# SyncE's issue order in two stretches of a one-core training step: stores between the late transposes of x, and transposes of phi(k) and dq around those of dk

## The chip, the core and the metric

The kernel runs on one NeuronCore of a Trainium2 chip. A core has five engines with a queue of instructions each: TensorE (PE, matrix multiplies, with its weight loads shown apart as PEld), VectorE (DVE), ScalarE (ACT), GpSimd (POOL) and SyncE (SP). SyncE computes nothing: it issues DMAs. An engine works through its queue in order, and an instruction whose semaphores are not there yet holds up all that stands behind it. The metric is the device time of one execution in microseconds (us); less is better.

## The reference

The step is the forward and backward pass of one pre-norm block with S = 2048 tokens, width D = 640, 32 heads of 20, and a feed-forward width F = 1728. Cut to what matters:

```python
phi = lambda t: jnp.where(t > 0, t + 1, jnp.exp(t)) + 1e-6
def A(x):                                   # linear attention
    q, k, v = heads(x @ wqkv)
    kv, z = sum_s(phi(k) v^T), sum_s(phi(k))
    return merge((phi(q) @ kv) / (phi(q) @ z + 1e-6)) @ wo
def B(x):                                   # gated feed-forward
    return (silu(x @ w_gate) * (x @ w_up)) @ w_down
h  = x + A(layernorm(x))
h2 = h + B(layernorm(h))
# returned: h2 and the gradients of x, wqkv, wo, w_gate, w_up, w_down for a given grad_out
```

Two products matter here. In the forward pass k and q come from `xn @ wqk`, where xn is the normalised x. In the backward pass the gradient of xn is a sum of three products, `dxn = dq @ Wq^T + phi(k) @ WV2 + dk @ Wk^T`. TensorE contracts over the partitions, so the left factor of each product is needed transposed (features on the partitions, tokens along the row): xnT for the first, dqT, pkT and dkT for the second.

## The kernel before, in words

The tokens are cut into 16 tiles of 128 (ST = 16), the width into 5 blocks of 128 (DT = 5). A result of one tile is 128x640, made in two halves of 320 columns (`NCH`). A manual schedule fixes the order of the code for all five engines in the first stretch below, and for SyncE and VectorE in the second; a scheduler orders the other engines there.

**The first stretch (lines 268 to 401).** For each tile t the kernel normalises x (`ln1_stats`, `ln1_xn` on VectorE and GpSimd), transposes it, and multiplies it by the k and q weights (`kq_mm`, line 299, with 20 matmuls a tile on line 305). Tiles 0 to 7 are transposed on TensorE (`ln1_tr`, `ln1_tr1`) and copied out. Tiles 8 to 15 are transposed by a DMA that SyncE issues: in the loop over t (line 369) the step t normalises tile t + 3 and issues its transpose (line 378). Between these transposes SyncE issues what the table `queue` (line 328) lists for step t, after that step's work: `load_dh2T` transposes rows of grad_out (lines 227 and 228), `store_q`, `store_k` and `store_x` write four tiles each of phi(q), phi(k) and xnT to DRAM for later stages (lines 319 to 326), and `load_wv`, `load_wo` and `load_wdT` fetch weights. One store moves 640 KB.

**The second stretch (lines 825 to 972).** Before its loop SyncE transposes weights (`wqkvT`, lines 840 and 745), and TensorE makes the rest of a sum for the attention output (`ps_gt`), the weight gradients `dwqk(0, i)` (line 883) and, in `wk2` (line 877), the five blocks of the matrix WK2, which SyncE transposes into WV2 (line 881). A buffer `ring` holds ten transposed tiles: four slots for dkT, three for pkT, three for dqT. `load_pqT(v)` (line 873) issues two DMA transposes, phi(k) of tile v from DRAM into slot 4 + v % 3 and dq of tile v from SBUF into slot 7 + v % 3:

```python
def load_pqT(v):
    nc.sync.dma_start_transpose(out=ring[:, 4 + v % 3], in_=scr_pk[v * P:(v + 1) * P, :])
    nc.sync.dma_start_transpose(out=ring[:, 7 + v % 3], in_=dq[v // 8][:, v % 8, :])
```

Lines 896 and 897 call it for tiles 0, 1 and 2 before any of that. The loop of line 927 then runs t from 0 to 18. At t < 16 it makes dk of tile t (`ps_dk`, ten matmuls through `mm_row` on line 109, finished on VectorE in lines 938 and 940) and issues its transpose on SyncE (line 941). Three steps later (LAG = 3, u = t - 3) it makes dxn of tile u (line 964): for each half five matmuls with dqT, five with pkT against WV2, and five with dkT, 30 in all. After them `load_pqT(u + 3)` reuses the slots just read (line 967). In the steps t = 2 and t = 3 stand also `dwqk(0, 3)` and `dwqk(0, 4)`. The layer norm's backward (`ln_bwd`) and the store of dx follow each dxn.

Everything else (the feed-forward's forward and backward pass, its weight gradients, the attention's backward pass, and the last products that make h2) is not touched.

Of the kernel before, what the change touches and what calls it, by code (L numbers as in the profile page):

```python
# [20 lines left out]
def kernel(  # L21
# [41 lines left out]
    def mm(name):  # L63

        return psum.tile([P, 2, 512], FP32, name=name, tag="mm")

    def row(ps):
        return ps[:, :, :320]

    def half(ap):  # L70
        return ap.rearrange("p (c n) -> p c n", c=2)
# [3 lines left out]
    def wk(name, w=D, pool=0):  # L75
        return wpools[pool].tile([P, w], BF16, name=name, tag="w", padded_shape=[P, D])
# [28 lines left out]
    def mm_row(ps, lhs, rhs, n, start=True, stop=True):  # L105

        for ci in range(2):
            for k in range(n):
                nc.tensor.matmul(ps[:, ci, :320], lhsT=lhs(k), rhs=rhs(k, *NCH[ci]),  # L109
                                 start=(start and k == 0), stop=(stop and k == n - 1))  # L110
# [31 lines left out]
    def ln_bwd(ps, xhat, rstd_col, resid, dst, pool):  # L142
        sums = small.tile([P, 2], FP32, name="lb_s", tag="lb_s")
        dy = wk("lb_dy", pool=pool)
        nc.scalar.activation(out=half(dy[:]), in_=row(ps), func=ACT.Copy, scale=rstd_col, accum_out=sums[:, 0:1])  # L145
        a = wk("lb_a", pool=pool)
        nc.vector.tensor_tensor_reduce(out=a[:], in0=dy[:], in1=xhat, scale=1.0, scalar=0.0,  # L147
                                       op0=ALU.mult, op1=ALU.add, accum_out=sums[:, 1:2])
        k = small.tile([P, 2], FP32, name="lb_k", tag="lb_k")
        nc.vector.tensor_scalar(out=k[:], in0=sums[:], scalar1=-1.0 / D, scalar2=None, op0=ALU.mult)  # L150
        nc.scalar.activation(out=a[:], in_=xhat, func=ACT.Identity, scale=k[:, 1:2], bias=k[:, 0:1])
        nc.vector.tensor_tensor(out=a[:], in0=a[:], in1=dy[:], op=ALU.add)
        nc.vector.tensor_tensor(out=dst, in0=a[:], in1=resid, op=ALU.add)
# [16 lines left out]
    def stage():  # L170
        return small.tile([P, 7, P], BF16, name="stg", tag="stg", bufs=3)
# [153 lines left out]
    def store_x(c):  # L325
        nc.sync.dma_start(out=scr_xnT[4 * c:4 * c + 4].rearrange("t p k c -> p t k c"), in_=xnT[:, 4 * c:4 * c + 4])

    queue = {4: [(load_dh2T, 0)], 5: [(store_q, 0)], 6: [(store_x, 0)], 7: [(load_dh2T, 512, 256)], 9: [(store_q, 1), (load_dh2T, 768, 256)],
             10: [(store_x, 1)], 11: [(store_k, 0)], 12: [(load_dh2T, 1024), (store_k, 1)], 13: [(store_x, 2), (load_wv,)],
             14: [(store_q, 2), (load_wo, 0, HG), (store_x, 3), (load_dh2T, 1536)],  # L330
             15: [(store_k, 2), (load_wdT, wdT, 1), (store_k, 3), (load_wdT, wdT3, 3)]}

# [139 lines left out]
    with tc.manual_schedule(engines={EngineType.PE, EngineType.DVE, EngineType.SP, EngineType.Pool}):  # L472
# [86 lines left out]
        for t in range(ST + 2):  # L559
# [19 lines left out]
            while h1_todo and h1_todo[0][0] < t:  # L579
                v, h1 = h1_todo.pop(0)  # L580
# [244 lines left out]
    with tc.manual_schedule(engines={EngineType.SP, EngineType.DVE}):  # L825
# [7 lines left out]
        def load_pk(t):  # L833
            pkrs[t] = small.tile([P, D], BF16, name="pkr", tag="stg", bufs=3, padded_shape=[P, 7 * P])
            nc.gpsimd.dma_start(out=pkrs[t][:], in_=scr_pk_v[:, t, :])
# [3 lines left out]
        def tr_cols(dst, src, c):  # L839
            nc.sync.dma_start_transpose(out=dst.unsqueeze(1), in_=src[:, c:c + P])  # L840
# [32 lines left out]
# [3 lines that stand above are left out]
# [7 lines left out]
        def dwqk(which, i, between=None):  # L883
            ev = wk("dwqk", pool=i % 2)
            ps = mm("ps_dwqk")
            for ci, (n0, n1) in enumerate(NCH):
                for t in range(ST):
                    nc.tensor.matmul(ps[:, ci, :320], lhsT=xn_r[:, t, i * P:(i + 1) * P],  # L888
                                     rhs=dq[t // 8][:, t % 8, n0:n1] if which == 0 else dk[:, t, n0:n1],
                                     start=(t == 0), stop=(t == ST - 1))  # L890
                if between and ci == 0:
                    between()
            nc.scalar.copy(out=half(ev[:]), in_=row(ps))
            nc.gpsimd.dma_start(out=out_2[i * P:(i + 1) * P, which * D:(which + 1) * D], in_=ev[:])

        for v in range(3):
            load_pqT(v)
        for t in range(ST):
            nc.vector.tensor_scalar(out=xn_r[:, t, :], in0=xn_r[:, t, :], scalar1=mv1[:, t, 0:1],
                                    scalar2=rstd1[:, t:t + 1], op0=ALU.subtract, op1=ALU.mult)  # L900
# [21 lines left out]
        def load_mT(t):  # L922
            if t % 4 == 0:
                mTs[t // 4] = strips.tile([P, 4, FT, P], BF16, name="mT", tag="S")
            nc.sync.dma_start_transpose(out=mTs[t // 4][:, t % 4], in_=scr_m[t * P:(t + 1) * P, :])

        for t in range(ST + LAG):
            if t in (2, 3):
                dwqk(0, t + 1)
            if t < ST:  # L930
                if t + 2 < ST:
                    load_pk(t + 2)
                pkr = pkrs.pop(t)
                nc.vector.tensor_scalar(out=pkr[:], in0=pkr[:], scalar1=-1e-6, scalar2=1.0, op0=ALU.add, op1=ALU.min)
                tk = wk("tk", pool=1)
                ps = mm("ps_dk")
                mm_row(ps, lambda i: xnT_r[:, t, i, :], lambda i, n0, n1: WK2[:, i, n0:n1], DT)
                nc.vector.scalar_tensor_tensor(out=half(tk[:]), in0=row(ps), scalar=rstd1[:, t:t + 1] if t < NC else 1.0,
                                               in1=half(dzb[:]), op0=ALU.mult, op1=ALU.add)
                nc.vector.tensor_tensor(out=dk[:, t, :], in0=tk[:], in1=pkr[:], op=ALU.mult)  # L940
                nc.sync.dma_start_transpose(out=ring[:, t % 4], in_=dk[:, t, :])
            if 8 <= t < 8 + HG:
                tr_cols(G[:, t - 8, :], scr_GT, OH[t - 8])
            if t == 14:
                nc.sync.dma_start_transpose(out=KV.rearrange("p j c -> p (j c)").unsqueeze(1), in_=scr_KVT)
            if t == ST:
                dKV = stage()[:, :HG, :]
                nc.sync.dma_start_transpose(out=dKV, in_=dKVT.rearrange("p j c -> p (j c)"))
            if t == ST:
                wd = big.tile([P, FT, D], BF16, name="wd", tag="B")  # L950
                nc.sync.dma_start(out=wd[:, :13, :], in_=B_w_down[0:13 * P, :].rearrange("(j p) d -> p j d", p=P))
                for r in (0, 64):
                    nc.sync.dma_start(out=wd[r:r + 64, 13, :], in_=B_w_down[13 * P:F, :])
            u = t - LAG
            if u < 0:
                continue
            if t >= ST:
                dwqk(1, t - ST)
            pkT, dqT, dkT = ring[:, 4 + u % 3], ring[:, 7 + u % 3], ring[:, u % 4]
            ps = mm("ps_dxn")  # L960
            for ci, (n0, n1) in enumerate(NCH):
                for k, (lhs, rhs) in enumerate(((dqT, wqkvT[:, 0:5]), (pkT, WV2), (dkT, wqkvT[:, 5:10]))):
                    for i in range(DT):
                        nc.tensor.matmul(ps[:, ci, :320], lhsT=lhs[:, i, :], rhs=rhs[:, i, n0:n1],  # L964
                                         start=(k == 0 and i == 0), stop=(k == 2 and i == DT - 1))
            if u + 3 < ST:
                load_pqT(u + 3)
            if ST - MTA <= u:
                load_mT(u - ST + MTA)
            dx = wk("dx")  # L970
            ln_bwd(ps, xn_r[:, u, :], rstd1[:, u:u + 1], dh1[:, u, :], dx[:], 0)
            nc.gpsimd.dma_start(out=o1_v[:, u, :], in_=dx[:])
# [120 lines left out]
```

## Time and profile before

| | |
|---|---|
| time, median of 4 runs | 813.49 us (812.93 to 815.82) |
| the profiled execution (one of the four) | 815.82 us |
| its span, first to last instruction | 814.1 us |
| granted TensorE clock | 1.000 |
| TensorE busy | 806.3 us (99%) |
| VectorE, ScalarE, GpSimd busy | 472.6 (58%), 286.1 (35%), 201.4 us (25%) |
| share of TensorE in the chain that ended last | 92% |
| DMA traffic | 159.79 MB, mean 196 GB/s |
| queue q1, which carries SyncE's DMAs | 83.43 MB, 55.8% of 16 engines' span |

The span is the time from the first to the last instruction; the profiled execution lasted 1.7 us longer than its span. A row of the timeline gives the start in us, the length in us, the engine, the line of the code, the operation and its operands as `out<-in`, a count, and in brackets how long the engine had stood idle and what released it. A row with SPq is a DMA being issued by SyncE, and its length is how long the issue kept SyncE, not how long the data took; that second time (from issue to landing) is listed with the DMA issues of a line or tile. The chain that ended last is followed back from the last instruction, at each step to what released it.

### The profile page before, as it was taken

Reading aid. Unit: us, or ns where it says so; the run is one execution under the profiler, and the core shown is the slowest. Engines: PE = TensorE matmul, PEld = TensorE weight load, DVE = VectorE, ACT = ScalarE, POOL = GpSimd, SP = SyncE. Lnnn points to the kernel's source line nnn. Section 1 sums busy time; section 2 is a strip of 40 time slices with the busy share of each in tenths; the row PEclk is TensorE's granted clock in tenths of the full one; section 3 lists DMA queues with packets and bytes.
Section 4 is the critical chain, followed back from the end, with each engine's and each line's share of the span. In section 5 each row is a group of like instructions: output and inputs, shape, how many; then the busy total and the mean of one; then the engine's idle time right before and its main releaser. Section 6 shows DMA issues by size and latency. Waiting matters only on the chain.

```text
span 814.1 us, 13781 instructions
## 1 busy us (share of the span) xinstructions
PE 806.3 (99%) x5436; PEld 518.2 (64%) x5436; DVE 472.6 (58%) x883; ACT 286.1 (35%) x400; POOL 201.4 (25%) x361
## 2 busy tenths in 40 slices
PE   9999999999999999999999999999999999999998
PEld 7766566555555555555666777777777677777676
DVE  7979988880095028710850158999897266631212
ACT  6962532750283035401831223223313133332010
POOL 4600045223422312121216201111211121112330
PEclk9999999999999999999999999999999999999999
DMA  9899899999778968991596857885599869999992
GB/s 251 182 284 254 170 248 259 193 255 221 182 164 212 210 173 174 236 247 50 136 243 172 279 126 195 221 199 163 128 201 188 167 131 167 169 237 198 201 278 88
DMA packets 281904, 159.79 MB, mean 196 GB/s; under 512 B 240220, under 2 KB 267997, under 8 KB 281840
## 3 DMA queue, kind: packets, MB, share of 16 engines
q1 hardware_dynamic: 256912, 83.43, 55.8%
q0 software_dynamic: 18416, 66.95, 26.7%
q10 hardware_dynamic: 6512, 8.54, 3.3%
q8 instruction: 42, 0.69, 0.4%
q14 instruction: 22, 0.18, 0.1%
HBM read 47.68 MB, written 53.66 MB: 124 GB/s over the span
## 4 chain that ended last, share of the span: by engine, by line
PE 92%; DVE 3%; DMA 3%; SPq 1%; POOL 0%; issue 0%; ACT 0%; DVEq 0%; POOLq 0%
PE ps_dw L705 22%; PE ps_dhn L109 14%; PE ps_dxn L964 8%; PE pu L638 7%; PE pg L633 7%; PE ps_o L1022 6%; PE ps_dm L411 5%; PE ps_dwqk L888 4%; PE ps_dp L109 3%; PE ps_gt L763 3%; PE ps_y L502 3%; PE ps_a L565 3%; PE ps_dk L109 2%; PE pdm L411 2%; PE ps_kq L305 2%; DMA h1r<-scr_h 2%
## 5 line engine op out<-in xcount | busy, mean ns | idle before, releaser
L109 PE MATMUL ps_dhn<-wgT,cols 128*128 128x320 bf16 x864 | 119.5, 299 | 0.0
L705 PE MATMUL ps_dw<-dd,hn 128*128 128x448 bf16 (+1 forms) x640 | 118.8, 346 | 0.0
L109 PEld LDWEIGHTS <-cols 128*128 128x128 bf16 x864 | 84.5, 98 | 32.9
L705 PEld LDWEIGHTS <-hn 128*128 128x128 bf16 x640 | 62.6, 98 | 54.2
L707 DVE CAST dwev<-ps_dw 128x896 bf16<-128x896 f32 (+3 forms) x12 | 10.9, 907 | 124.5 <-PE ps_dw L705 109.6
L670 POOL DMA_DIRECT2D scr_dT<-stg x64 | 34.6, 541 | 165.4 <-DMA stg<-dd 163.9
L707 ACT CAST dwev<-ps_dw 128x896 bf16<-128x896 f32 (+1 forms) x20 | 17.6, 878 | 159.0 <-PE ps_dw L705 150.6
L147 DVE CUSTOM_DVE_ANT_0 lb_a<-lb_dy,hn 128x640 bf16<-128x640 bf16 x32 | 26.4, 825 | 66.8 <-ACT lb_dy L145 66.8
L638 PE MATMUL pu<-wgu,hnT 128*128 128x448 bf16 (+1 forms) x320 | 63.6, 346 | 0.0
L633 PE MATMUL pg<-wgu,hnT 128*128 128x448 bf16 (+1 forms) x320 | 63.6, 346 | 0.0
L1022 PE MATMUL ps_o<-wd,mT 128*128 128x320 bf16 (+3 forms) x462 | 61.1, 295 | 0.0
L705 PE MATMUL ps_dw<-m_s,dh 128*128 128x448 bf16 (+1 forms) x320 | 60.4, 346 | 0.0
L964 PEld LDWEIGHTS <-ring 128*128 128x128 bf16 x480 | 46.9, 98 | 20.5 <-DMA ring<-dk 2.3
L964 PE MATMUL ps_dxn<-wqkvT,ring 128*128 128x320 bf16 x320 | 51.3, 299 | 2.0 <-DMA ring<-dk 2.0
L1022 PEld LDWEIGHTS <-mT 128*128 128x128 bf16 (+1 forms) x462 | 41.8, 97 | 17.5 <-issue 2.6
L638 PEld LDWEIGHTS <-hnT 128*128 128x128 bf16 x320 | 31.3, 98 | 27.1
L705 PEld LDWEIGHTS <-dh 128*128 128x128 bf16 x320 | 31.3, 98 | 27.1
L633 PEld LDWEIGHTS <-hnT 128*128 128x128 bf16 x320 | 31.3, 98 | 27.0
L411 PEld LDWEIGHTS <-dh2T 128*128 128x128 bf16 x320 | 31.0, 98 | 25.1
L411 PE MATMUL ps_dm<-wdT,dh2T 128*128 128x448 bf16 (+1 forms) x240 | 46.5, 344 | 0.0
L305 PE MATMUL ps_kq<-wqk,xnT 128*128 128x320 bf16 x320 | 45.0, 299 | 0.8 <-DMA xnT<-xn 0.7
L145 ACT ACTIVATE lb_dy<-ps_dhn,rstd 128x640 bf16<-128x640 f32 x16 | 12.7, 794 | 87.4 <-PE ps_dhn L109 87.4
(167 smaller groups left out, 1303.8 us busy)
## 6 DMA issues: line engine op xcount, KB each, us to landing
scr_dT<-stg POOLq DMA_DIRECT2D x48, 224.0 KB, 3.1
cols<-scr_dT POOLq DMA_DIRECT2D x6, 1728.0 KB, 8.1
scr_m<-m_s POOLq DMA_DIRECT2D x12, 448.0 KB, 4.7
cols<-scr_dT ACTq DMA_DIRECT2D x2, 1728.0 KB, 9.9
out_dram<-dwev POOLq DMA_DIRECT2D x30, 112.0 KB, 2.2
scr_dT<-stg POOLq DMA_DIRECT2D x16, 192.0 KB, 2.6
scr_pq<-pqa SPq DMA_DIRECT2D x4, 640.0 KB, 4.2
scr_xnT<-xnT SPq DMA_DIRECT2D x4, 640.0 KB, 5.4
```

What stands on the lines that cost most here:

```text
L109: nc.tensor.matmul(ps[:, ci, :320], lhsT=lhs(k), rhs=rhs(k, *NCH[ci]), start=(start and k == 0), stop=(stop and k == n - 1))
L147: nc.vector.tensor_tensor_reduce(out=a[:], in0=dy[:], in1=xhat, scale=1.0, scalar=0.0, op0=ALU.mult, op1=ALU.add, accum_out=sums[:, 1:2])
L305: nc.tensor.matmul(ps[:, ci, :320], lhsT=xnT[:, t, k, :], rhs=wqk[:, k, w0 + n0:w0 + n1], start=(k == 0), stop=(k == DT - 1))
L411: nc.tensor.matmul(ps[:, c, :w], lhsT=dh2T[:, kt, (t + c) * P:(t + c + 1) * P], rhs=wdT[:, kt, o:o + w], start=(kt == 0), stop=(kt == DT - 1))
L633: nc.tensor.matmul(pg[:, c, :w], lhsT=hnT[:, kt, (t + c) * P:(t + c + 1) * P], rhs=wg[:, kt, 0:w], start=(kt == 0), stop=(kt == DT - 1))
L638: nc.tensor.matmul(pu[:, c, :w], lhsT=hnT[:, kt, (t + c) * P:(t + c + 1) * P], rhs=wg[:, kt, w:2 * w], start=(kt == 0), stop=(kt == DT - 1))
L670: nc.gpsimd.dma_start(out=scr_dT[t + c, :, KO[g]:KO[g] + GK[g], :], in_=stg[:, :GK[g], :])
L705: nc.tensor.matmul(ps[:, c, :w], lhsT=lhs(t), rhs=rhs(t), start=(t == 0), stop=(t == ST - 1))
L707: last = copy(out=ev[:, :len(parts), :w], in_=ps[:, :len(parts), :w])
L888: nc.tensor.matmul(ps[:, ci, :320], lhsT=xn_r[:, t, i * P:(i + 1) * P], rhs=dq[t // 8][:, t % 8, n0:n1] if which == 0 else dk[:, t, n0:n1] ...
L964: nc.tensor.matmul(ps[:, ci, :320], lhsT=lhs[:, i, :], rhs=rhs[:, i, n0:n1], start=(k == 0 and i == 0), stop=(k == 2 and i == DT - 1))
L1022: nc.tensor.matmul(po(t, ci), lhsT=mTs[t // 4][r, t % 4, j, :], rhs=wd[r, j, n0:n1], start=(t, ci) not in opened, stop=last)
```

## The change

Two lists are reordered, and nothing is added or taken away: SyncE has the same 174 rows of DMAs and the same bytes before and after; no other engine's order changes.

In the table `queue` four stores move. `store_x(1)` moves from step 10 to step 8, so it is issued between the transposes of tiles 11 and 12 and no longer between those of tiles 13 and 14. `store_q(1)` moves from step 9, and `store_k(0)` from step 11, to step 12 behind `load_dh2T(1024)`, which is behind the transpose of tile 15. `store_k(1)` moves from step 12 to step 13. Between the transposes of tiles 12 and 13 there remains `load_dh2T(768, 256)`, and between those of tiles 13, 14 and 15 nothing.

In the second stretch `load_pqT` is called for tile 0 alone before the loop. Tile 1's two transposes are issued behind the transpose of dk of tile 0, and tile 2's behind that of dk of tile 1. SyncE's order there was: pk, dq of tiles 0, 1, 2; the five transposes of WK2; dk of tiles 0, 1, 2, 3. It becomes: pk, dq of tile 0; the five of WK2; dk 0; pk, dq 1; dk 1; pk, dq 2; dk 2; dk 3.

```diff
     queue = {4: [(load_dh2T, 0)], 5: [(store_q, 0)], 6: [(store_x, 0)],
-             7: [(load_dh2T, 512, 256)], 9: [(store_q, 1), (load_dh2T, 768, 256)],
-             10: [(store_x, 1)], 11: [(store_k, 0)], 12: [(load_dh2T, 1024), (store_k, 1)], 13: [(store_x, 2), (load_wv,)],
+             7: [(load_dh2T, 512, 256)], 8: [(store_x, 1)],
+             9: [(load_dh2T, 768, 256)], 12: [(load_dh2T, 1024), (store_q, 1), (store_k, 0)], 13: [(store_k, 1), (store_x, 2), (load_wv,)],
              14: [(store_q, 2), (load_wo, 0, HG), (store_x, 3), (load_dh2T, 1536)],
              15: [(store_k, 2), (load_wdT, wdT, 1), (store_k, 3), (load_wdT, wdT3, 3)]}
...
-        for v in range(3):
-            load_pqT(v)
+        load_pqT(0)
...
                 nc.sync.dma_start_transpose(out=ring[:, t % 4], in_=dk[:, t, :])
+                if t < 2:
+                    load_pqT(t + 1)
```

More of the change, by code (lines that the diff above doesn't have):

```diff
@@ L326, in store_x @@
         nc.sync.dma_start(out=scr_xnT[4 * c:4 * c + 4].rearrange("t p k c -> p t k c"), in_=xnT[:, 4 * c:4 * c + 4])
-    queue = {4: [(load_dh2T, 0)], 5: [(store_q, 0)], 6: [(store_x, 0)], 7: [(load_dh2T, 512, 256)], 9: [(store_q, 1), (load_dh2T, 768, 256)],
-             10: [(store_x, 1)], 11: [(store_k, 0)], 12: [(load_dh2T, 1024), (store_k, 1)], 13: [(store_x, 2), (load_wv,)],
+    queue = {4: [(load_dh2T, 0)], 5: [(store_q, 0)], 6: [(store_x, 0)], 7: [(load_dh2T, 512, 256)], 8: [(store_x, 1)],
+             9: [(load_dh2T, 768, 256)], 12: [(load_dh2T, 1024), (store_q, 1), (store_k, 0)], 13: [(store_k, 1), (store_x, 2), (load_wv,)],
              14: [(store_q, 2), (load_wo, 0, HG), (store_x, 3), (load_dh2T, 1536)],
```

## The prediction, made before the changed kernel ran

> **What bounds the kernel now.** I read the page's busy shares first: TensorE is busy 806.3 of 814.1 us at a granted clock of 1.000, and the chain that ended last lies on it for 92%. Such a kernel gets faster only by fewer matmuls or by fewer gaps on TensorE, and this change removes no matmul. So the second view is who TensorE waited for:
>
> ```profile
> PE ps_dxn L964 <- DMA ring<-dk: 2.0, 1, 2.0
> PE ps_warm L341 <- POOL ident masks.py:199: 1.6, 1, 1.6
> PE ps_kq L305 <- DMA xnT<-xn: 0.7, 1, 0.7
> PE ps_dwo L983 <- DVE h1r L1029: 0.5, 1, 0.5
> ```
>
> The columns are total us, times, longest. Four waits, each met once; the first and the third are for DMAs that SyncE issues in the two stretches of the change. Nothing else in those stretches can be won: 2.0 + 0.7 = 2.7 us is the ceiling. The third view is the timeline of SyncE around each. First the x transposes:
>
> ```profile
> 31.84 1.42 SPq L228 DMA_TRANSPOSE dh2T<-in_grad_out_dram  x1
> 33.35 3.19 SPq L378 DMA_TRANSPOSE xnT<-xn  x2
> 36.67 0.49 SPq L323 DMA_DIRECT2D scr_pq<-pqa  x1
> 37.22 1.97 SPq L228 DMA_TRANSPOSE dh2T<-in_grad_out_dram  x1
> 39.28 1.23 SPq L378 DMA_TRANSPOSE xnT<-xn  x1
> 40.56 0.57 SPq L326 DMA_DIRECT2D scr_xnT<-xnT  x1
> 41.23 1.87 SPq L378 DMA_TRANSPOSE xnT<-xn  x1
> 43.15 0.99 SPq L320 DMA_DIRECT2D scr_pk<-pk  x1
> 44.23 2.88 SPq L378 DMA_TRANSPOSE xnT<-xn  x1
> ```
>
> Counted from the first at 24.61, the two at 33.35 are tiles 11 and 12, then come 13 (39.28), 14 (41.23) and 15 (44.23). The chain in order of time says which one was late:
>
> ```profile
> 41.23 6.42 DMA xnT<-xn
> 47.65 0.05 issue
> 47.69 5.61 PE ps_kq L305 x40
> ```
>
> Forty matmuls are two tiles, so TensorE stood before tile 14. Its transpose, issued right behind `store_x(1)`, landed after 6.42 us; tile 13's, with no store right before it, took 3.3. Now the second stretch:
>
> ```profile
> 625.42 2.30 SPq L874 DMA_TRANSPOSE ring<-scr_pk  x1
> 627.77 1.27 SPq L875 DMA_TRANSPOSE ring<-dq  x1
> 629.09 1.31 SPq L874 DMA_TRANSPOSE ring<-scr_pk  x1
> ...
> 634.52 6.59 SPq L881 DMA_TRANSPOSE wvk<-wvk  x5
> 641.21 5.92 SPq L941 DMA_TRANSPOSE ring<-dk  x4
> ...
> 645.47 1.53 PE L964 MATMUL ps_dxn<-wqkvT,ring 128*128 128x320 bf16 x10 [1.97 <-DMA ring<-dk]
> ```
>
> SyncE never pauses from 625.42 to 647.13. VectorE had finished dk of tile 0 by 630.89, yet its transpose is issued at 641.21 and lands 4.2 us later, at 645.4. TensorE wants it at 645.47 - 1.97 = 643.50. The queue is what is late, not the data.
>
> **Part 1: pk and dq of tiles 1 and 2 behind dk of tiles 0 and 1.** The four issues from 629.09 leave the place before WK2's five. Their cost there is the start of the five minus their own, 634.52 - 629.09 = 5.43 us. Do the five have another reason to wait? The last block of WK2 is copied out by ScalarE at 625.03 + 1.29 = 626.3, and the GpSimd DMAs that the first of them also waits for are old loads of `cols` into the reused buffer, long landed. So they start at 629.1. By their own row, and the gap after it, they take 641.21 - 634.52 = 6.69 us; dk 0 is issued at 635.8 and lands, at 4.2 us, at 640.0: 3.5 us before TensorE asks. The wait of **1.97 us** goes whole.
>
> What is late next: WV2's last block was issued at 639.89 and landed 4.3 us later, at 644.2; it is now issued at 634.5 and is no wait. What stands behind the moved issues: with 1.3 us an issue, pk 1 and dq 1 go at 637.1 and 638.4, dk 1 at 639.7, pk 2 and dq 2 at 641.1 and 642.4, dk 2 at 643.7, dk 3 at 645.0. Without its wait dxn 0 ends at 648.36 - 1.97 = 646.39, ten dk matmuls (1.36) follow, and dxn 1 opens at 647.75: dq 1 has landed at 642.8 if I allow 4.4 us. dkT of tile 1 is wanted two groups later at 649.1 and lands at 644.1. Tile 2 opens 5.44 us later, at 653.2; its dq lands at 646.8, its dk at 648.1. Tile 3's pk and dq wait for TensorE to leave their slots, as before; SyncE now ends dk 3 at 646.2 instead of 647.13. VectorE finishes dk 1, 2 and 3 at 632.45, 637.9 and 643.5, before each is issued, so no new wait on VectorE holds SyncE. Everything from there is paced by TensorE.
>
> Bounds: an issue has cost 1.2 to 2.3 us in this stretch. At 2.3 the five of WK2 take 11.5 us, dk 0 is issued at 640.6 and lands at 644.8; 0.7 us would be won. I take 1.97, since the five themselves cost 1.32 each.
>
> [...]
>
> **Part 2: stores between the x transposes.** Until 34.6 us nothing changes. Then `store_x(1)` (0.57 us of SyncE) goes ahead of tile 12, whose xn is ready at 34.91 + 0.40 = 35.31 anyway: it is issued at 35.35 instead of about 35.3. `load_dh2T(768, 256)` follows at about 37.2 and tile 13 at about 39.2, as before; tile 14 at 40.7 (its xn is ready at 40.68) instead of 41.23, with no store ahead of it; tile 15 at 42.9 instead of 44.23. Tile 14 then lands, at 3.3 to 4.8 us (the rows of tiles 9 to 13 but for 12's 2.6), at 44.0 to 45.5; TensorE asks at 47.69 - 0.69 = 47.00. Its wait of 0.69 us goes. Tile 15 lands by 42.9 + 5.7 = 48.6 at the latest row; TensorE asks at 49.7.
>
> But tile 12 now stands where 14 stood, behind a store. TensorE asks for it two tiles (2 x 2.72) before 47.00, at 41.55. Two rows bound its landing: tile 10, behind `store_x(0)`, took 4.8 us, and tile 14 6.4. So it lands at 40.15 to 41.75: 1.4 us early to 0.2 late. Tile 14's row is nearer, because the same load of dh2T and a transpose ran ahead of it (37.22 and 39.28 there, 31.84 and 33.35 here). I take 0.2 lost, and 0.69 - 0.2 = **0.49 us** won. Tile 13 may be held up too: landing at 39.2 + 4.4 = 43.6, it meets its 44.27.
>
> The stores moved back cost what stands behind them. `load_dh2T(1024)` goes earlier, at about 45 against 47.17. `store_q(1)` and `store_k(0)` then put 1280 KB and two issues of 0.5 to 1.0 us ahead of `load_wv`, `load_wo` and `load_dh2T(1536)`. At the longest store of this stretch, 8.3 us, these come at most 16.6 us later. The tightest of them, dh2T(1536), landed at 60.96 + 7.4 = 68.4, and the seventh dm step asks for it at 89.5; 21 us of slack cover it. The readers of the stores themselves come hundreds of us later. No GpSimd or ScalarE queue is passed.
>
> **The sum.** 1.97 + 0.49 = 2.46 us. TensorE is gapless from 47.69 to 641.97, so I let the gain through unchanged. Against the profiled execution it is 815.82 - 2.46 = 813.36 us. That execution was the slowest of four; against the median, which I forecast, 813.49 - 2.46 = **811.0 us**. The bound of 0.3%, about what a measurement of this kernel can tell from no change, is 2.44 us: the forecast lies on it.
>
> **Rivals.**
> 1. Only part 1 pays: tile 12's wait takes tile 14's place in full (landing 7.1 us after issue or more). For it: DMA share 0.95 from 24 to 47 us. Against: tile 10's 4.8. Gain 1.97, 811.5 us.
> 2. The change doesn't do what it says: dk 0 stays late, since the DMA engines and not SyncE set the pace of transposes (first row 2.30 us). Gain 0.7 + 0.49 = 1.2, 812.3 us. Against it: five issues of 1.32.
> 3. Given back at the end: TensorE waits 0.5 us at 759 us for h1r, whose load took 12.59 us. If those DMAs keep their own time, the gain comes back as a longer wait there: 813.5 us. Against it: their issues follow GpSimd's store of dx, which follows TensorE.
> 4. Slower: the store ahead of tile 12 clogs. From a landing after 41.55 + 2.66 = 44.21, 8.9 us behind its issue, the new wait eats both that it replaced; the longest store, 8.3 us, and one transpose of 1.2 behind it give 34.6 + 9.5 = 44.1. With a second such store (`store_x(0)` not yet drained) tile 12 would land some 3 us later and the time be 816 us. Against it: `store_x(0)` landed in 3.8 us.
>
> **Chances.** Forecast (gain 2.3 to 2.9, time 810.6 to 811.2) 0.64; rival 1 0.16; rival 2 0.07; rival 3 0.06; rival 4 0.07. Faster by over 0.3%: 0.55 out of the forecast's 0.64, since tile 10's row would give the full 2.66 us. Slower by over 0.3%: most of rival 4, 0.05. The rest, 0.40, is within 0.3%. The range 809.8 to 813.2 leaves out rival 4, rival 3 and a little at each end: 813.49 - 2.66 less the 0.56 by which the fastest run lies under the median is 810.3, and less the 0.5 of h1r's wait 809.8; rival 2 with a scatter of 0.4, and its further loss of part 2's 0.49, gives 813.2.
>
> **What would show it.** Part 1 right: no wait of ps_dxn for ring; dk 0 issued near 636 (shifted by part 2's gain). Part 2 right: no wait of ps_kq at tile 14 and at most 0.2 us at tile 12. Wrong: a wait over 0.5 us on line 305 at 41.5 us, issues of over 2 us on line 881, a longer wait for h1r, or busy TensorE time that grows.

## The result and the profile after

| | before | changed |
|---|---|---|
| median | 813.23 us (79 runs) | 812.17 us (51 runs) |
| lowest | 812.2 us | 811.7 us |
| the profiled execution | 815.82 us, span 814.1 | 812.70 us, span 811.0 |
| ratio, 95% interval | | 0.9983 (0.9976 to 0.9991) |

The change makes the kernel faster by 0.17%, some 1.1 to 1.4 us, which is inside the stated range and about half of the forecast 2.46 us. Executions that were disturbed are left out of the ratios. The two profiled executions differ by 3.1 us, far more than the medians; that difference is the subject of this study.

The waits of TensorE in the changed kernel (total us, times, longest):

```profile
PE ps_warm L341 <- POOL ident masks.py:199: 1.6, 1, 1.6
PE ps_dw L705 <- DMA dh<-in_grad_out_dram: 0.3, 1, 0.3
```

Both waits that the change aimed at are gone, and so is the 0.5 us for h1r, which the change doesn't touch; a new one of 0.3 us stands at the first weight gradient. Removed and added sum to 2.0 + 0.7 + 0.5 - 0.3 = 2.9 of the 3.1 us.

SyncE's timeline of the changed kernel, first stretch:

```profile
34.09 1.23 SPq L378 DMA_TRANSPOSE xnT<-xn  x1
35.41 0.53 SPq L326 DMA_DIRECT2D scr_xnT<-xnT  x1
36.03 1.92 SPq L378 DMA_TRANSPOSE xnT<-xn  x1
38.00 1.61 SPq L228 DMA_TRANSPOSE dh2T<-in_grad_out_dram  x1
39.71 5.33 SPq L378 DMA_TRANSPOSE xnT<-xn  x3
```

The last row is tiles 13, 14 and 15 back to back. Tile 12, behind the store, was issued at 36.03 and landed 4.4 us later, at 40.4; tile 14 at 41.0 + 4.8 = 45.8. TensorE's matmuls of this stretch end at 52.54 without a gap, so it asked for tile 12 at 52.54 - 4 x 2.72 = 41.66 and for tile 14 at 47.10. Both had more than 1 us to spare.

Second stretch of the same timeline, and the chain there:

```profile
626.49 1.28 SPq L874 DMA_TRANSPOSE ring<-scr_pk  x1
...
629.25 6.65 SPq L881 DMA_TRANSPOSE wvk<-wvk  x5
636.00 1.25 SPq L940 DMA_TRANSPOSE ring<-dk  x1
...
639.98 1.22 SPq L940 DMA_TRANSPOSE ring<-dk  x1
```

```profile
640.46 1.36 PE ps_dk L109 x10
641.82 4.08 PE ps_dxn L965 x30
645.89 1.36 PE ps_dk L109 x10
```

The reader should see the five transposes of WK2 pulled forward to 629.25, dk of tile 0 behind them at 636.00 (5.2 us earlier than before), and the thirty matmuls of dxn 0 in one piece.

### The profile page after: what moved, and what is told of

It reads as the page before. It is cut to its first block, busy times and chain, and to the rows that moved or that the text cites. A ratio compares the mean times of both kernels' runs of the same rounds, so it can differ in the third digit from the quotient of the medians.

```text
span 811.0 us, 13780 instructions
## 1 busy us (share of the span) xinstructions
PE 806.2 (99%) x5436; PEld 518.7 (64%) x5436; DVE 473.0 (58%) x883; ACT 286.0 (35%) x400; POOL 201.4 (25%) x361
## 4 chain that ended last, share of the span: by engine, by line
PE 96%; DMA 3%; DVE 0%; issue 0%; ACT 0%; POOL 0%; POOLq 0%
PE ps_dw L705 21%; PE ps_dhn L109 14%; PE ps_dxn L965 8%; PE ps_o L1023 7%; PE pg L633 6%; PE ps_kq L305 5%; PE ps_dwqk L888 5%; PE ps_dm L411 5%; PE pu L638 5%; PE ps_gt L763 3%; PE ps_dp L109 3%; PE ps_y L502 3%; PE ps_dk L109 3%; PE ps_a L565 3%; DMA stg<-dd 2%; PE pdm L411 2%
## 5 line engine op out<-in xcount | busy, mean ns | idle before, releaser
L705 PEld LDWEIGHTS <-hn 128*128 128x128 bf16 x640 | 62.6, 98 | 54.2
L707 DVE CAST dwev<-ps_dw 128x896 bf16<-128x896 f32 (+3 forms) x12 | 10.9, 908 | 130.5 <-PE ps_dw L705 109.6
L965 PE MATMUL ps_dxn<-wqkvT,ring 128*128 128x320 bf16 x320 | 51.3, 299 | 0.0
L1030 DVE TENSOR_TENSOR h1r<-ps_o,h1r 128x640 bf16<-128x640 f32 x15 | 12.1, 823 | 52.6 <-PE ps_o L1023 52.6
```

Of the source, the lines that this page charges most:

```text
L705: nc.tensor.matmul(ps[:, c, :w], lhsT=lhs(t), rhs=rhs(t), start=(t == 0), stop=(t == ST - 1))
L707: last = copy(out=ev[:, :len(parts), :w], in_=ps[:, :len(parts), :w])
```

## The experiments

**Theory A**: the two waits are what the change removes, but their size varies from execution to execution, and the profiled one of before had them large. **Theory B**: they are as large in nearly every execution, and the changed kernel loses some 1.3 us elsewhere, as at the load of dh. The first four runs, on one chip, divide the change and repeat both ends.

**Part 1 alone** (before, with the edit of `load_pqT`; the table `queue` as before).

> Only the second stretch is changed (pk and dq of tiles 1 and 2 behind dk of tiles 0 and 1); the stores between the x transposes stay as before. Theory A (the two waits are real, but their size varies from execution to execution and the profiled one of before had them large): no wait of ps_dxn for ring, the wait of ps_kq for xnT stays (0 to 0.9 us), and the median lies 0.5 to 1.2 us under before's. Theory B (each wait is 2.0 and 0.7 us in nearly every execution, and the changed kernel loses some 1.3 us in another place, as at the load of dh): this part alone wins its full 2.0 us, or loses part of it to a new wait that its profile shows.

Measured: median 812.95 against 813.48 us, ratio 0.9986 (0.9972 to 1.0). No wait for ring, 0.5 us for xnT. The slowest of its 12 executions took 813.74; before's reached 817.78.

**Part 2 alone** (before, with the new table `queue`; `for v in range(3): load_pqT(v)` stays).

> Only the stores between the x transposes are moved; pk and dq of tiles 1 and 2 stay ahead of dk. Theory A: no wait of ps_kq, the wait of ps_dxn for ring stays with a size other than 1.97 us by over 0.3, and the median lies 0.2 to 0.7 us under before's. Theory B: the wait of ps_dxn is 1.8 to 2.2 us again, and the median is the same as before's or up to 0.7 us under it, with a wait for dh at the first ps_dw of up to 0.7 us.

Measured: median 812.73 us, ratio 0.9984 (0.9968 to 1.0001). Its profiled execution had no wait for xnT and 2.2 us for ring, near the 1.97 of before, as theory B had it. But that execution took 816.50, and seven of the twelve took 812.2 to 812.8: they can't have waited 2.2 us. The wait is sometimes there and sometimes not.

**Before again.**

> The kernel before once more, for a second profile and as a control of the comparison: ratio 1.000 with an interval of about 0.001 to each side. Theory A: its waits of ps_dxn for ring and of ps_kq for xnT sum to 1.0 to 1.8 us. Theory B: they sum to 2.4 to 3.0 us, as in the first profile.

Measured: median 814.09 us, ratio 1.0011 (0.9993 to 1.003), so the comparison is good to about 0.2% (1.6 us) here, and the 0.5 and 0.8 us by which the medians of the two parts lay under before's are inside that. The waits in this second profile of the unchanged kernel:

```profile
PE ps_dxn L964 <- DMA ring<-dk: 1.2, 1, 1.2
PE ps_kq L305 <- DMA xnT<-xn: 0.6, 2, 0.3
```

Together 1.8 us, the upper edge of what theory A had, against 2.7 in the first, and none for h1r.

**The changed kernel again.**

> The changed kernel once more, for a second profile on the same chip as its two parts: 0.7 to 2.0 us under before. Theory A: TensorE's gaps sum to 2 us or less, of which 1.6 are at the start. Theory B: a gap of 0.5 us or more in a place where before has none (the load of dh at 175 us, or h1r at 755 us).

Measured: median 812.41 us, ratio 0.9975 (0.9959 to 0.999). TensorE waits 1.6 us at the start and nowhere else; the wait for dh isn't there. This execution is the median one of its twelve, so theory B has no place left where 1.3 us could be lost, and falls. Theory A says that the wait varies but not why. In six profiles SyncE reached pk of tile 0 anywhere between 620.85 and 626.49 us. What stands ahead of it are 16 transposes of weights, and the first six of them are slow. From the timeline of SyncE in the kernel before:

```profile
588.95 1.21 SPq L783 DMA_TRANSPOSE dh1T<-dh  x1
590.21 20.57 SPq L840 DMA_TRANSPOSE wqkvT<-in_A_wqkv_dram  x6
610.82 14.56 SPq L745 DMA_TRANSPOSE wqkvT<-in_A_wqkv_dram  x10
```

Six took 20.57 us and the next ten 14.56. One issue, at 593.3, held SyncE for 10.9 us, while GpSimd's four loads of xnT_r (640 KB each, from 590 us on) were landing, 15.4 us after issue in the median. In the second profile of the changed kernel those loads took 10.4, and the longest issue 7.6. **Theory J** (jam): these loads decide how late SyncE is, and so whether dk of tile 0 is late. **Rival Q**: only the number of transposes counts. Four more runs on a second chip:

**Before, with the jam taken away**: three of the four loads go into the loop (`load_xnT_r` issues the same load, but tied to its place in GpSimd's order).

```diff
-        for c in range(4):
-            pool_load(xnT_r[:, 4 * c:4 * c + 4], ...)
+        load_xnT_r(0)
...
             if t in (2, 3):
                 dwqk(0, t + 1)
+            if t in (0, 2, 5):
+                load_xnT_r({0: 1, 2: 2, 5: 3}[t])
```

> The kernel before, but of the four loads of xnT_r (640 KB each, GpSimd, at 590 us) only the first stays there; the other three are issued in the loop over t, at t = 0, 2 and 5. Theory J (jam): the size of the wait for ring is set by how long SyncE's transposes of the weights wqkvT are held up by these loads (third issue 7.6 to 10.9 us in the profiles so far). Then that issue falls under 4 us, SyncE reaches pk of tile 0 before 620 us, ps_dxn doesn't wait for ring, and the median lies 0.3 to 1.2 us under before's, with part 1 of the change not made. Rival Q (the number of transposes alone): the loads don't matter, the wait stays between 1.2 and 2.2 us and the median is before's.

Its timeline of SyncE:

```profile
588.44 1.21 SPq L783 DMA_TRANSPOSE dh1T<-dh  x1
589.70 10.71 SPq L840 DMA_TRANSPOSE wqkvT<-in_A_wqkv_dram  x6
```

The longest of the six issues is now 2.2 us, pk of tile 0 goes out at 615.84, and ps_dxn doesn't wait for ring, though all six transposes of pk and dq still stand ahead of dk. Rival Q falls on this. The median, 813.09 against 813.91 us, is of the right size, but its ratio, 0.9989 (0.9963 to 1.0015), doesn't settle it; one of its executions took 823.17 us and was not profiled.

**The changed kernel, with the jam taken away** (the same edit).

> The changed kernel with the same three loads of xnT_r issued later. Theory J: no wait for ring here either, so part 1 of the change is worth nothing once the jam is gone; what is left between this kernel and the last one is part 2, 0.3 to 0.7 us. Rival Q: this kernel is 1.7 to 2.7 us under the last one.

Measured: 812.19 us, ratio 0.9962 (0.9945 to 0.9978), no wait but the first. It lies 0.9 us under the last kernel, a little more than the 0.3 to 0.7 that theory J had and about half of the 1.7 that rival Q needs at least.

**A dose**: before, with pk and dq of tiles 1 and 2 transposed twice.

```diff
-        for v in range(3):
+        for v in (0, 1, 2, 1, 2):
             load_pqT(v)
```

> The kernel before with pk and dq of tiles 1 and 2 transposed a second time ahead of WK2's five: four more issues, 5.3 us of SyncE, ahead of dk of tile 0. Theory J: executions differ in where the queue stands; those with a long jam wait the 5.3 us in full, those with a short one had 1 to 3 us to spare and wait 2 to 4.5 us; the median rises by 3.0 to 4.8 us. Rival Q: every execution of before waits about 2 us already, so the median rises by 5.1 to 5.5 us.

Measured: median 820.45 us, 6.5 over before's 813.91, with a ratio of 1.006 (1.0034 to 1.0086): more than either theory had. The profiled execution, one of the fastest at 816.49, waited 3.3 us for ring, in line with theory J: SyncE was early (pk of tile 0 at 621.12), and 5.3 - 3.3 = 2.0 us of the dose went into spare time. What the others lost beyond 5.3 us is the question of the next run of this kernel.

**One store of part 2**: `store_x(1)` alone moved from step 10 to step 8.

> The kernel before with store_x(1) alone moved from step 10 to step 8; store_q(1) and store_k(0) stay. If the store right ahead of tile 14's transpose is the whole cause of the wait of ps_kq: tile 14 lands in under 5 us and the waits of ps_kq sum to 0.1 us or less; the median lies 0.3 to 0.7 us under before's. Rival (the sum of the bytes of the stores between 36 and 44 us is the cause): a wait of 0.3 us or more is left, at tile 14 or at tile 15 behind store_k(0).

Measured: 813.94 us, ratio 0.9992 (0.9973 to 1.0011). Its waits:

```profile
PE ps_kq L305 <- DMA xnT<-xn: 1.1, 1, 1.1
PE ps_dxn L964 <- DMA ring<-dk: 0.9, 1, 0.9
```

The chain puts the first before 60 matmuls, three tiles: the wait moved from tile 14 to tile 13 and grew.

```profile
40.36 4.86 DMA xnT<-xn
45.22 0.04 issue
45.27 8.32 PE ps_kq L305 x60
```

Tile 13 has no store right ahead of it, but `store_q(1)` and a transpose of dh2T before that. It was issued at 40.36 instead of 39.28, since SyncE reached it later, and it landed after 4.9 us instead of 3.3. So the store right ahead is not the whole cause. The queue of stores costs twice here, 1.1 us in SyncE's time and 1.6 in the landing; this run does not separate the stores' bytes from their order.

The last four runs (the dose had a single execution), on a third chip:

**The dose again**, for its profile.

> The kernel of the doubled transposes once more, for one more profile. Its times stood in steps (815.8 to 816.5, 817.9 to 818.7, 820.4 to 821.8 and 822.9 us) that go with the mean granted clock of the execution (1.000, 0.998, 0.996, 0.994). Theory H: a late dk costs twice, once as the wait of ps_dxn for ring (3 to 5.5 us) and again because the granted clock falls to 0.50 for stretches of about 3.4 us around it, each worth 1.7 us of busy TensorE time. Then this profile, if its clock is under 0.999, shows one or more such stretches between 640 and 665 us and TensorE busy time 1.7 us over 806.3 for each. Rival: the lower clock is met at another place, and the step with it has nothing to do with dk.

This execution took 819.83 us at a mean clock of 0.996. Windows of 2 us (start:end, length, busy us and number of instructions of PE, PEld, DVE, ACT and POOL, then granted clock, DMA share, GB/s):

```profile
645.00:647.00 2.00, 0.00 (x0) 0.00 (x0) 0.00 (x0) 0.00 (x0) 0.00 (x0) 0.80 1.12 119
647.00:649.00 2.00, 1.08 (x5) 0.62 (x6) 0.00 (x0) 0.00 (x0) 0.00 (x0) 0.50 0.82 161
...
651.00:653.00 2.00, 2.00 (x10) 1.10 (x8) 0.00 (x0) 0.00 (x0) 0.00 (x0) 0.50 0.00 0
653.00:655.00 2.00, 2.00 (x16) 1.46 (x15) 0.70 (x1) 0.89 (x2) 0.00 (x0) 1.00 0.55 114
```

```profile
647.92 2.85 PE L964 MATMUL ps_dxn<-wqkvT,ring 128*128 128x320 bf16 x10 [4.29 <-DMA ring<-dk]
```

The clock falls at about 646.2, while TensorE still waits for ring, and stays at half until 653: ten matmuls in 2 us where it later does sixteen. From 630 to 645 us and from 653 to 700 it is 1.00, and the execution's mean of 0.996 leaves no room for another such stretch: 6.8 us at half clock are 3.4 of its 818.1 us, 0.004. This answers the rival. So theory H holds for this execution: the late dk cost 4.3 us of waiting and about 2.5 us more at half clock from 647.9 to 653, which together are the 6.8 us that it lies over before's median of 813.03 on this chip. In one point theory H was off: the half clock lasted 6.8 us, two of its stretches, but part of it fell into the wait, so the span less TensorE's waits rose to 818.1 - 7.3 = 810.8 us (808.5 to 809.6 in the profiles with a clock of 0.999 or 1.000), by 1.2 to 2.3 us and not by 1.7 us for each. Two more waits stand near the kernel's start. One, 0.8 us of ps_kq, is put down to ScalarE, but tile 14's transpose landed at 41.25 + 6.5 = 47.75, 0.75 us after the 47.00 at which TensorE asked for it in the first profile: by that it is the wait for xnT again. The other, 0.6 us before a transpose of x on TensorE, was met in this execution alone.

**Two stores of part 2**: `store_q(1)` and `store_k(0)` to step 12, `store_x(1)` left at step 10. `store_k(1)` goes to step 13 with them, as in the change.

> The kernel before with store_q(1) and store_k(0) alone moved to step 12; store_x(1) stays between the transposes of tiles 13 and 14. If all three stores count through their bytes (the reading after the last experiment): tile 14 lands at 4.0 to 5.5 us behind store_x(1), the waits of ps_kq sum to 0.3 us or less. If the store right ahead is the cause: 0.5 us or more at tile 14 as in before. The median is 0 to 0.7 us under before's.

Measured: no wait of ps_kq at all; tile 14, 1.3 us behind the store, landed 5.3 us after issue. Ten of twelve executions took 811.85 to 813.57 us, and the median is 812.18, the changed kernel's own; two took 818.77 and 822.25 with clocks of 0.998 and 0.996, which holds the ratio at 0.9998 (0.9971 to 1.0026). With `store_q(1)` gone tile 14 was also issued earlier, at 40.40 instead of 41.23. So part 2 works through these two stores; as far as this profile and the median show, moving `store_x(1)` as well isn't needed.

**The changed kernel a third time, and once more without the jam.**

> The changed kernel on the same chip as the next run: 0.7 to 2.0 us under before; TensorE's waits in its profile 2.1 us or less in all, 1.6 of them at the start; no execution with a clock under 0.999 but for one in twelve.

> The changed kernel with the three loads of xnT_r issued in the loop, once more, beside the changed kernel: the question is whether it beats both. If the changed kernel's transposes keep their 3.5 us to spare in nearly every execution, the medians agree within 0.3 us and only the slowest executions differ; if the jam still costs the changed kernel something, this one is 0.3 to 0.8 us faster in the median.

Measured: 812.08 us, ratio 0.9979 (0.9961 to 0.9997), and 812.17 us, ratio 0.9983 (0.9968 to 0.9997). Moving the loads of xnT_r doesn't beat the changed kernel. All 24 executions of that version stay under 812.8 us, while the changed kernel had two of 75 over 814, too few to tell the two apart.

One table takes the profiles together. "dk 0" is the time from SyncE's issue of the last dh1T to its issue of dk of tile 0; "loads" is the median landing of the loads of xnT_r issued near 590 us (four, or the one that is left where the jam was taken away); "wait" is that of ps_dxn for ring.

| kernel | loads | dk 0 | wait |
|---|---|---|---|
| before | 15.4 | 52.3 | 2.0 |
| before again | 15.3 | 51.3 | 1.2 |
| store_x alone | 14.6 | 51.2 | 0.9 |
| part 2 alone | 15.7 | 52.1 | 2.2 |
| two stores | 9.8 | 47.9 | 0 |
| before, no jam | 7.8 | 42.9 | 0 |
| dose | 9.3 | 53.2 | 3.3 |
| dose again | 10.7 | 54.2 | 4.3 |
| part 1 alone | 11.2 | 43.5 | 0 |
| changed (three profiles) | 15.6, 10.4, 16.1 | 47.4, 43.0, 47.9 | 0, 0, 0 |
| changed, no jam (two) | 8.0, 9.5 | 42.0, 42.0 | 0, 0 |

The wait is what dk 0 exceeds 50.1 by, to 0.3 us in every row; 50.1 is fitted to the six rows with a wait. Four loads land in 9.3 to 11.2 us (a short jam) or in 14.6 to 16.1 us (a long one), under the changed order as under the old. Without a dose the old order waited in its four profiles of the second kind and not in the one of the first (two stores). Why an execution falls into the one or the other was not found.

## Why the prediction was right or wrong

The mechanism was right in part 1 and half right in part 2, and the range held the time; the size was off. The step that failed is the end of part 1, "The wait of **1.97 us** goes whole", as a gain on the median. It does go whole, but 1.97 us was one execution's wait. Other executions of the old order waited 2.2, 1.2, 0.9 and 0 us, and the one profiled first was the slowest of its four, 2.3 us over their median. The prediction noted that and carried its waits over to the median all the same.

**Part 1's timetable.** dk of tile 0 was to be issued at 635.8, dk 1 at 639.7, dk 2 at 643.7; measured 636.00, 639.98 and 644.79. The 3.5 us to spare were worked out from an execution with a long jam; with dk 0 at 47.4 to 47.9 in such executions the table leaves 2.2 to 2.7, because pk 0 went out later there, 37.9 us behind the last dh1T (626.49 - 588.63) in the first profile of the changed kernel against 36.5 in before. What the working left out is what stands ahead of 625 us. It took the start of pk 0 as given, where this start varies by more than the wait.

**Part 2.** The choice between tile 10's 4.8 us and tile 14's 6.4 for a landing behind a store went to the wrong row: tile 12 landed after 4.2 to 4.6 us in six profiles, and the 0.2 us was not lost. The wait that part 2 removes was there in all six profiles that keep the old table: 0.7, 0.6, 0.5, 0.6, 0.7 and 0.8 us (the last is the one put down to ScalarE); no profile with the new table has it. The reason given, the store right ahead of tile 14, is only part of it: the two runs that move some of the stores show that the queue of all of them counts.

**The sum on the median.** Part 2's 0.5 to 0.8 us of waiting and the 0.5 us that part 1 alone gave in the median, its wait being nil in many executions, make 1.0 to 1.3; 1.1 to 1.4 were measured. The forecast's 2.46 is near what an execution like the profiled one gains; the two profiled ones differ by 3.1, 0.5 of it from h1r's wait, which the change doesn't touch.

**Rivals.** Rival 1 (only part 1 pays) did not come true: part 2 pays as well. In the median the two alone gave 0.5 and 0.8 us on the first chip, which the intervals don't tell apart, and on the third the two stores of part 2 alone reached the changed kernel's median. Rival 2's 812.3 us is nearer to the measured 812.17 than the forecast, but by luck: its condition, a late dk 0, was met in no profile with part 1. It named the DMA engines as what sets the pace of transposes. Something of the kind holds for the six weight transposes ahead, which GpSimd's loads slow down (20.57 us in before, 10.71 with three of the four loads moved), though not for WK2's five, which take 6.5 to 6.7 us in long-jam profiles. Rival 3 (h1r) and rival 4 (a clog at tile 12) were not met. The forecast's own 810.6 to 811.2 us, given 0.64, was missed, and so was faster by over 0.3%, given 0.55: the time moved by 0.17%.

**What was missed on the other side** is the tail. On the three chips of the experiments 42 of 108 executions of before took over 814 us, and 14 had a mean clock of 0.998 or less (817.3 to 819.8 us). Of the 60 executions of kernels with part 1 on the same chips (part 1 alone, the changed kernel, and both runs of it without the jam) one took over 814 us, and none had such a clock. Elsewhere the changed kernel had one, 820.95 us at 0.996, so part 1 does not rule them out. Part 1 is thus worth about 0.5 us in the median and more in the long executions. Half clock around a late dk was not seen in a profile of before itself, but in two of its relatives (3.4 us of it in part 2 alone, 6.8 in the dose). A late dk can't be the whole account: before without the jam, whose profile has dk 7 us early, had an execution of 823.17 us at 0.993 that was not profiled.

## What to carry to other kernels

A wait in one profile is the wait of one execution: look how that execution stands to the median, and follow the late queue back to where its own start varies, before a wait is carried to the median as a gain. When an in-order queue is late, ask what held it earlier, not only what stands directly ahead; here four loads of another engine, issued some 50 us before dk 0, decided it (dk 0 went out at 42.9 us in the table with three of them moved, at 47.9 to 52.3 in the old order with all four). A transpose that nothing needs soon belongs behind one that is needed, even when the profile at hand shows time to spare, since a wait on TensorE may cost more than its length: here 4.3 us of waiting came with some 2.5 us more at half clock.

## What the runs showed of the hardware

**A wait of 2.2 us on TensorE was followed by half clock.** In the profiled execution of part 2 alone the wait and the windows of 1 us behind it read (columns as above):

```profile
645.14 2.38 PE L964 MATMUL ps_dxn<-wqkvT,ring 128*128 128x320 bf16 x10 [2.16 <-DMA ring<-dk]
```

```profile
645.00:646.00 1.00, 0.86 (x6) 0.57 (x7) 0.00 (x0) 0.00 (x0) 0.00 (x0) 0.83 1.07 223
646.00:647.00 1.00, 1.00 (x5) 0.59 (x4) 0.00 (x0) 0.00 (x0) 0.00 (x0) 0.50 0.75 138
...
649.00:650.00 1.00, 1.00 (x9) 0.70 (x8) 0.00 (x0) 0.21 (x1) 0.00 (x0) 0.96 0.00 0
```

The clock is 0.50 from about 645.7 to 649.1, some 3.4 us; the span less TensorE's waits is 814.8 - 3.8 = 811.0 us, 1.4 to 2.5 us more than in the profiles with a clock of 0.999 or 1.000. It does not follow each wait: 2.0 us in the first profile of before and 3.3 in the dose's left it at 1.00, while the 4.3 us of the dose's second profile brought half clock from about 646.2 to 653, some 6.8 us. The dose's twelve executions stand in steps with the mean clock: 815.8 to 816.5 us at 1.000, 817.9 to 818.7 at 0.998, 820.4 to 821.8 at 0.996, 822.9 at 0.994. So the length of a wait alone does not tell whether half clock follows: 2.2 us was followed by it once, 3.3 us in another execution was not. What else decides it was not shown.

**An issue on SyncE was held for 10.9 us while another engine's loads were landing.** Of the six transposes of L840 near 590 us the shortest took 1.3 us to issue in ten profiles. The longest took 6.6 to 10.9 us in the nine of these with GpSimd's four loads there, and 2.2 us in the one with a single load (before, no jam). All six together took 15.7 to 21.5 us in the eleven profiles with four loads and 10.7 to 12.5 in the three with one.
